# A new order in the front of a long-convolution and MLP kernel: load queues, a masked table, turns and norms on another engine, and both column means ahead of one stage

## The chip, the cores and the metric

The kernel runs on one core of a Trainium2 chip. A core has five engines that work side by side, each through its own list of instructions in order: TensorE (PE, matrix products into PSUM; its weight loads are shown as PEld), VectorE (DVE), ScalarE (ACT), GpSimd (POOL) and SyncE (SP). SyncE and ScalarE also issue DMA transfers; the two queues are shown as SPq and ACTq. Instructions wait for each other through semaphores.

The metric is the device time of one execution in microseconds (us), as the median of several runs. A profiled execution has its own time, and a span from its first to its last instruction.

## The reference, cut to what matters

```python
def _A_ref(q, k, v, shift_k, ssm_k, ssm_D):     # q: layernorm of the input x
    # k_shift: causal convolution of k along the sequence with 4 taps a channel
    for t in range(ks):
        k_shift = k_shift + k_pad[:, t:t + S, :] * shift_k[:, ks - 1 - t][None, None, :]
    kv = k_shift * v
    # y: causal convolution of kv along the sequence with ssm_k (by FFTs of length 2S), a channel each
    y = y + kv * ssm_D[None, None, :]
    return q * y

def _B_ref(x, w1, w2):
    return relu(x @ w1) @ w2

x = A_q
h = x + _A_ref(_layernorm(x), A_k, A_v, A_shift_k, A_ssm_k, A_ssm_D)
h2 = h + _B_ref(_layernorm(h), B_w1, B_w2)      # S = 2048, D = 512, Dff = 1376, bf16
```

## The kernel before

The convolution of length 4096 is done as a transform in two stages of matrix products with tables of sines, a product of spectra, and an inverse transform. The order on each engine is the order of the calls in the source (`tc.manual_schedule()`); there is no planner.

**Loads.** `load_rows(eng, rg)` loads `ssm_k`, 128 channels as a group `rg`, in two pieces of 256 KB (d = 0, 1) into the tile `kfl` in runs of 64 bf16. Group 1 and later group 3 go through ScalarE's queue, behind the small `wsh` (the 4 taps) and `drow` (ssm_D); groups 0 and 2 go through SyncE's queue. Then SyncE's queue carries, in this order: four transposing loads `kT` of `k` (`load_k`, L140 to L146), `vfl` (L112 to L116), the first rows of x (`qn0`, L161 to L163) between them, and `w1` (L154 to L159).

**Tables.** `f1f` is a small table of sines (ScalarE, L179) for stage 1. It is split in a bf16 high part `f1hi` and a low part `f1lo` (VectorE, L242 to L244), which GpSimd copies into `f1w` (`paired`, L253 to L257): a table that has the four groups of 32 partitions in one or the other of two column blocks, zero elsewhere. `drow2` (`spikes`) has ssm_D in the same layout. The larger table `tab` of stage 2 has 32 x 4 x 64 entries a partition: blocks 0 and 1 are sines of "turns" (`turns2`: integers on VectorE, a multiplication with addition at L184 and a mask at L185, then `sines2` on ScalarE); blocks 2 and 3 are their negatives (`negated`, GpSimd, L276). `inverse_turns` prepares tables of the inverse transform on GpSimd, `diagonals` the diagonal matrices `wdiag` of the 4 taps.

**Front.** `warm(13, ...)` runs products whose result nobody uses (L421). `s1(gb)` is stage 1 of ssm_k for one eighth of the channels: 4 products that add the spike of ssm_D (L350), 32 products on `kfl` and `f1w` (L358), and two copies out of PSUM, one on ScalarE and one on VectorE ("AD": first half on ACT, second on DVE; L317, L319). `tap(u)` is the 4-tap convolution of a chunk of k (L375) with a copy to `ksh`. `second_k(kp)` is stage 2 of ssm_k for a pair of frequencies (L388), with a copy back into `a1k` by the engine its letter names. It reads blocks 0 to 2 of `tab`; the products of x (`product`) also read block 3. All of these take PSUM tiles through `bank2`, in a fixed rotation of four tiles: the fourth tile before must have been copied out.

`row(q)` transposes a quarter of `ksh` (L333) and multiplies it by v into `xfl` (VectorE, L335). `bn_stats`, `moments` and `norm_rows(0, ...)` give the first layernorm of x. `column_means(m)` sums columns of w1 by products (L408), ScalarE copies them to `wm` (L410) and `center(n)` subtracts them from w1 on GpSimd (L414). Then stage 1 of x (`stage1(... xfl ...)`, L546) runs in eight steps, with the second half of the means and centers behind its first step.

**After that.** `product(kp)`, 16 times: two stage-2 products `u2` and `u1`, then the spectra are multiplied, `u2` on VectorE (L575), `u1` on GpSimd from a copy by ScalarE (L574, L580) for ten of the sixteen and on VectorE for the others. The inverse transform, the gate, the second layernorm and the MLP (`mlp1`, `mlp2`) follow.

Of the kernel before, what the change touches and what calls it, by code (L numbers as in the profile page):

```python
# [9 lines left out]
ALU = mybir.AluOpType  # L10
# [5 lines left out]
P = 128  # L16
# [39 lines left out]
def kernel(  # L56
# [37 lines left out]
    def first_channel(rg, d):  # L94
        return 128 * rg + 64 * (d ^ (rg % 2))
# [5 lines left out]

    kfl = front.tile([P, 64, 2, 64], BF16, name="kfl")

    def load_rows(eng, rg):
        for d in range(2):
            src = bass.AP(tensor=A_ssm_k.tensor, offset=A_ssm_k.offset + S * first_channel(rg, d), ap=[[64, 32], [S, 64], [1, 64]])
            eng.dma_start(out=kfl[32 * rg:32 * rg + 32, :, d, :], in_=src)


    vfl = front.tile([P, 64, P], BF16, name="vfl")  # L110

    def load_v(r):  # L112
        for d in range(2) if r % 2 else (0,):
            n = 64 if r % 2 else P
            src = bass.AP(tensor=A_v.tensor, offset=A_v.offset + first_channel(r, d), ap=[[64 * D, 32], [D, 64], [1, n]])
            nc.sync.dma_start(out=vfl[32 * r:32 * r + 32, :, 64 * d:64 * d + n], in_=src)  # L116

    zero = consts.tile([P, 512], BF16, name="zero")
    nc.vector.memset(zero[:], 0.0)
# [14 lines left out]
    def chunk(name):  # L134
        return front.tile([P, DC, CH + 16], BF16, tag="kT", name=name, bufs=4)


    tb = [chunk(f"tb{b}")[:].rearrange("p c t -> p (c t)").bitcast(I32)[:, 0:1024].rearrange("p (a b) -> p a b", b=64) for b in range(2)]

    def load_k(c):  # L140
        kT[c] = chunk("kT")
# [77 lines left out]
    f1f = early.tile([P, 64], F32, name="f1f")  # L219
    _sin(f1f[:, 0:32], t1[:, 0:32], 128)  # L220
    _sin(f1f[:, 32:64], t1[:, 32:64], 128, neg=True)
    load_rows(nc.scalar, 3)
    o2 = consts.tile([P, 2, 2], F32, name="o2")
    for i in range(2):
        for b in range(2):
            nc.vector.tensor_scalar(out=o2[:, i, b:b + 1], in0=n2c[:], scalar1=32.0 * i, scalar2=4096.0 + 2048.0 * b,
                                    op0=ALU.mult, op1=ALU.add)

    def turns2(i, b):
# [4 lines left out]
    ta00 = turns2(0, 0)  # L234
    ta01 = turns2(0, 1)
    f1hi = consts.tile([P, 64], BF16, name="f1hi")
    f1lo = consts.tile([P, 64], BF16, name="f1lo")
    f1d = early.tile([P, 64], F32, name="f1d")


    tab = tabp.tile([P, 32, 4, 64], F32R, name="tab")
# [27 lines left out]

    wm = rows.tile([P, 4, 344], F32, name="wm")  # L270

    def sines2(i, b, ta):
        _sin(tab[:, 16 * i:16 * i + 16, b, :], ta, 8192)
# [144 lines left out]
    def warm(n, data=zero[:], lhsT=None):  # L418
        ps = bank2("warm")
        for i in range(n):  # L420
            nc.tensor.matmul(out=ps[:, i % 2, :], lhsT=data[:, 0:P] if lhsT is None else lhsT, rhs=data, start=True, stop=True)  # L421
# [29 lines left out]
    def norm_rows(q, out, src):  # L451
        for i in range(4):
            t = 4 * q + i
            nc.vector.tensor_scalar(out=out[:, i, :], in0=src[:, i, :], scalar1=mv1[:, t, 0:1],
                                    scalar2=rstd1[:, t, :], op0=ALU.subtract, op1=ALU.mult)

    xfl = None
# [20 lines left out]
    spikes()  # L478
    sines2(0, 0, ta00)
    ta10 = turns2(1, 0)  # L480
    sines2(0, 1, ta01)
    ta11 = turns2(1, 1)
    diagonals()
    paired()
    negated(0)
    negated(1)
    sines2(1, 0, ta10)
    sines2(1, 1, ta11)
    load_k(2)
    load_k(3)  # L490
    load_v(0)
    load_v(2)
    load_x0()
    load_v(1)
    load_v(3)
    load_w1()
    negated(2)
    negated(3)
# [12 lines left out]
    tap(2, "A")  # L511
    second_k(0, "A")
    second_k(1, "D")
    second_k(2, "A")
    tap(3, "A")
    second_k(3, "D")
    second_k(4, "A")
    tap(4, "A")
    second_k(5, "D")
    pairs_pool()  # L520
    second_k(6, "A")
    tap(5, "D")
    nc.vector.bn_stats(out=st[:, 0, :], in_=qn0[:, 0, :])
    second_k(7, "A")
    tap(6, "A")
    nc.vector.bn_stats(out=st[:, 1, :], in_=qn0[:, 1, :])
    second_k(8, "A")
    tap(7, "D")
# [24 lines left out]

    late = pl.push("late")
# [300 lines left out]
```

## Time and profile before

| what | us |
|---|---|
| median of 3 runs (201.39 to 201.84) | 201.69 |
| the profiled execution's own time | 200.89 |
| its span | 199.1 |
| PE busy | 171.6 |
| DVE busy | 146.3 |
| ACT busy | 98.9 |
| POOL busy | 90.7 |

The chain that ended last, followed back from the last instruction, is TensorE for 66% of the span, VectorE for 21%, 5% "issue" (time in which an engine waited for nothing that the profile shows) and ScalarE for 3%. A mean over the whole span hides the stages: the MLP at the end is TensorE alone, while the front passes from loads to products to copies. So the views by time say more here than the totals: the chain in order of time, the timeline of an engine or a queue in a window, and the packets of a DMA queue in a window. In a chain line the columns are start, duration, engine, output tile, source line and count. In a timeline line they are start, duration, engine, line, operation, output and input tiles, count, and in brackets the idle time before it with what ended it.

### The profile page before, as it was taken

The page shows a single profiled execution, that of the slowest core. Times are in us where ns is not written, and L with a number is a line of the kernel's source. Part 1 is how long each engine was busy: PE and PEld are TensorE (multiplying, and loading weights), DVE is VectorE, ACT ScalarE, POOL GpSimd, SP SyncE. Part 2 cuts the span into 40 slices and gives each one's busy share as a digit, 9 for nine tenths or more (in the row PEclk, how much of TensorE's full clock was granted, in tenths as well). Part 3 has the DMA queues.
Part 4 walks back from the last instruction along what each step waited for, and adds up shares of the span by engine and source line. Part 5 has one row for each costly group of instructions (what it writes and reads, how often), then busy time and mean ns, then how long its engine had stood idle before and what let it go on. Part 6 is the DMA issues. An engine that isn't in the chain of part 4 may idle for free.

```text
span 199.1 us, 4079 instructions
## 1 busy us (share of the span) xinstructions
PE 171.6 (86%) x1638; PEld 109.1 (55%) x1643; DVE 146.3 (73%) x258; ACT 98.9 (50%) x113; POOL 90.7 (46%) x108
## 2 busy tenths in 40 slices
PE   0389989898986888888966999999999999999992
PEld 0137866496775777757744745445454444444451
DVE  7967866998667999999999869979966570471142
ACT  0387688931786588814995478003630164036300
POOL 7999983121991999992985520220220020002000
PEclk9999999999999999999999999999999999999999
DMA  7999998980000000008802622302511271120022
GB/s 117 216 242 198 193 203 133 203 174 0 3 3 3 0 5 0 3 0 221 200 0 53 201 86 44 59 12 64 112 29 26 61 102 27 40 58 8 3 54 53
DMA packets 51379, 15.99 MB, mean 80 GB/s; under 512 B 46784, under 2 KB 50208, under 8 KB 51360
## 3 DMA queue, kind: packets, MB, share of 16 engines
q1 hardware_dynamic: 42464, 14.61, 36.0%
q10 hardware_dynamic: 8896, 1.12, 3.7%
q8 instruction: 13, 0.21, 0.5%
q14 instruction: 6, 0.05, 0.1%
HBM read 9.64 MB, written 2.10 MB: 59 GB/s over the span
## 4 chain that ended last, share of the span: by engine, by line
PE 66%; DVE 21%; issue 5%; ACT 3%; ACTq 2%; POOL 1%; DVEq 0%; POOLq 0%
PE m L725 19%; PE m L780 18%; DVE a1x L575 7%; PE ps L358 6%; DVE zs L618 5%; PE u L388 4%; PE pkv L375 3%; PE ps2k L388 3%; PE pz L645 3%; PE warm L421 3%; DVE a1k L580 3%; PE pi L613 2%; ACT a1x L317 2%; DVE xfl L335 2%; PE pz L655 2%
## 5 line engine op out<-in xcount | busy, mean ns | idle before, releaser
L761 ACT ACTIVATE h1T<-m 128x512 bf16<-128x512 f32 (+1 forms) x44 | 25.9, 597 | 43.5 <-PE m L725 43.5
L725 PE MATMUL m<-hT,w 128*128 128x512 bf16 (+1 forms) x176 | 39.0, 379 | 0.2 <-ACT hT L692 0.2
L780 PE MATMUL m<-w,h1T 128*128 128x512 bf16 (+1 forms) x161 | 36.1, 379 | 0.2
L786 DVE SCALAR_TENSOR_TENSOR o<-m,rstd,hp 128x128 bf16<-128x128 f32 (+1 forms) x48 | 15.8, 389 | 25.6 <-PE m L780 24.8
L448 POOL TENSOR_SCALAR rstd<-mv 128x4 f32<-128x4 f32 x8 | 1.9, 232 | 64.4 <-DVE mv L446 64.4
L725 PEld LDWEIGHTS <-w 128*128 128x128 bf16 (+1 forms) x176 | 17.4, 100 | 20.5 <-issue 0.5
L780 PEld LDWEIGHTS <-h1T 128*128 128x128 bf16 (+1 forms) x165 | 15.9, 98 | 19.3 <-issue 0.3
L580 POOL TENSOR_TENSOR a1k<-usb,a1k 128x1024 fp32r<-128x1024 f32 x10 | 23.7, 2391 | 5.0 <-DVE a1x L575 5.0
L388 PE MATMUL u<-a1x,tab 64*128 64x256 f32 x256 | 18.8, 288 | 4.9 <-DVE a1k L580 2.4
L626 ACT CAST a1x<-zs 128x1024 fp32r<-128x1024 f32 (+2 forms) x10 | 17.3, 1730 | 10.8 <-DVE zs L618 10.8
L575 DVE TENSOR_TENSOR a1x<-u,a1k 128x1024 fp32r<-128x1024 f32 x16 | 19.1, 1218 | 2.7 <-PE u L388 2.7
L388 PEld LDWEIGHTS u<-a1x,tab 64*128 64x128 f32 x256 | 16.4, 185 | 6.9 <-PE u L388 3.1
L624 POOL CAST a1x<-zs 128x1024 fp32r<-128x1024 f32 (+1 forms) x8 | 15.7, 1975 | 7.6 <-DVE zs L618 7.6
L618 DVE STREAM_TRANSPOSE zs<-pi 128x1024 f32<-128x1024 f32 x16 | 18.4, 1216 | 0.5 <-PE pi L613 0.5
L613 PE MATMUL pi<-a1k,wd 128*128 128x512 f32 x32 | 13.3, 417 | 2.6 <-DVE zs L618 1.5
L414 POOL TENSOR_TENSOR w<-w,wm 128x1376 bf16<-128x1376 bf16 x4 | 11.2, 2839 | 6.5 <-ACT wm L410 6.5
L317 ACT CAST a1k<-ps2k 128x1024 fp32r<-128x1024 f32 x12 | 11.9, 1016 | 4.2 <-PE ps2k L388 4.1
L574 ACT COPY usb<-u 128x1024 f32<-128x1024 f32 x10 | 10.1, 1016 | 5.9 <-PE u L388 5.6
L613 PE MATMUL pi<-a1x,wd 128*128 128x512 f32 x32 | 12.8, 400 | 0.0
L319 DVE CAST a1k<-ps 128x1024 fp32r<-128x1024 f32 x8 | 9.6, 1223 | 4.2 <-PE ps L358 4.2
L421 PE MATMUL warm<-zero,wdiag 128*128 128x512 bf16 x13 | 5.1, 581 | 8.4 <-DVE drow L251 8.4
L388 PE MATMUL ps2k<-a1k,tab 64*128 64x256 f32 x128 | 10.5, 296 | 1.4 <-DVE a1x L575 0.8
(116 smaller groups left out, 278.3 us busy)
## 6 DMA issues: line engine op xcount, KB each, us to landing
xall<-in_A_q_dram SPq DMA_DIRECT2D x16, 128.0 KB, 3.5
out_dram<-o SPq DMA_DIRECT2D x62, 32.0 KB, 1.6
w<-in_B_w_dram SPq DMA_DIRECT2D x4, 344.0 KB, 6.1
w<-in_B_w_dram SPq DMA_DIRECT2D x1, 1280.0 KB, 6.4
kfl<-in_A_ssm_k_dram SPq DMA_DIRECT2D x4, 256.0 KB, 5.4
kfl<-in_A_ssm_k_dram ACTq DMA_DIRECT2D x4, 256.0 KB, 6.4
vfl<-in_A_v_dram SPq DMA_DIRECT2D x2, 512.0 KB, 7.3
vfl<-in_A_v_dram SPq DMA_DIRECT2D x4, 256.0 KB, 4.9
```

What stands on the lines that cost most here:

```text
L317: nc.scalar.copy(out=o, in_=i)
L388: nc.tensor.matmul(out=ps[:, d, 256 * i:256 * i + 256], lhsT=tab[rw, k1, b:b + 2, :].rearrange("p b k -> p (b k)"), rhs=a_in[rw, c, k1, :] ...
L575: nc.vector.tensor_tensor(out=spot(a1x, kp), in0=u2[:], in1=kk.bitcast(F32), op=ALU.mult)
L580: (nc.gpsimd if pool else nc.vector).tensor_tensor(out=kk, in0=(usb if pool else u1)[:], in1=kk.bitcast(F32), op=ALU.mult)
L613: nc.tensor.matmul(out=ps[:, b, :], lhsT=wd[:, m:m + 2, :].rearrange("p b k -> p (b k)"), rhs=src[:, d, 16 * b:16 * b + 16, c0:c0 + 32], s ...
L618: nc.vector.transpose(out=zs[:], in_=ps[:].rearrange("p b (k c) -> p c (b k)", c=32))
L624: nc.gpsimd.tensor_copy(out=o, in_=i)
L626: nc.scalar.copy(out=o, in_=i)
L725: nc.tensor.matmul(out=ps1[:fsz].rearrange("p (i t) -> p i t", i=4), lhsT=w1[:, c, fc * P:fc * P + fsz], rhs=hT[sc][:, c // 2, :, c % 2, : ...
L761: nc.scalar.activation(out=h1T[:fsz, fc, :], in_=ps1[:fsz], func=ACT.Relu)
L780: nc.tensor.matmul(out=ps2[:], lhsT=lhsT, rhs=w2[:ksz, fc, :], start=(fc == 0), stop=(fc == NFC - 1))
L786: nc.vector.scalar_tensor_tensor(out=of(o[:], d)[:, a], in0=ps[:, a], scalar=rstd2[:, t, :], in1=pair(hp[sc][:, d, i, :])[:, a], op0=ALU.m ...
```

## The change

Nine things, in the front alone:

1. `load_rows` takes one piece (d) at a time. ScalarE's queue begins with piece (1, 1), then `drow`, then (1, 0); behind the two activations of `f1f` it goes on with (3, 1), `wsh`, (3, 0). SyncE's queue begins with (0, 0), as before, and keeps its order.
2. A tile `pad` of 112 bf16 in `consts` makes up for tiles that went and came, so that the tiles behind it keep their addresses (`kfl` is at 40192, a multiple of 256, before and after).
3. `f1w` and `drow2` are made on VectorE by multiplication with a mask of two columns, in place of `f1hi`, `f1lo`, `f1d` and nine GpSimd operations and four VectorE copies.
4. The turns of the second half of `tab` (i = 1) are made on GpSimd, with the mask still on VectorE, in between stage 1's copies; their sines come in between the copies of `second_k`. They have a tile `tt` of their own instead of two of the `kT` buffers.
5. `negated` makes one block at a time; block 3 comes after the moments, block 2 where `second_k` needs it.
6. `inverse_turns` comes ahead of `diagonals` on GpSimd; the warm-up has 14 products on `f1w`.
7. The taps and `second_k` stand in another order, with other engines for their copies.
8. `norm_rows(0, ...)` runs on GpSimd.
9. `column_means(1)` and the centers 2 and 3 come ahead of the first step of x's stage 1.

```diff
-    def load_rows(eng, rg):
-        for d in range(2):
-            src = bass.AP(tensor=A_ssm_k.tensor, offset=A_ssm_k.offset + S * first_channel(rg, d), ap=[[64, 32], [S, 64], [1, 64]])
-            eng.dma_start(out=kfl[32 * rg:32 * rg + 32, :, d, :], in_=src)
+    def load_rows(eng, rg, d):
+        src = bass.AP(tensor=A_ssm_k.tensor, offset=A_ssm_k.offset + S * first_channel(rg, d), ap=[[64, 32], [S, 64], [1, 64]])
+        eng.dma_start(out=kfl[32 * rg:32 * rg + 32, :, d, :], in_=src)
...
-    nc.vector.memset(drow2[:], 0.0)
-    nc.scalar.dma_start(out=wsh[:], in_=A_shift_k.rearrange("(r p) j -> p r j", p=P))
+
+    consts.tile([P, 112], BF16, name="pad")
+    load_rows(nc.scalar, 1, 1)
+    load_rows(nc.sync, 0, 0)
     nc.scalar.dma_start(out=drow[0:P:16, :], in_=A_ssm_D.rearrange("(r g) -> r g", g=64))
-    load_rows(nc.scalar, 1)
-    for rg in (0, 2):
-        load_rows(nc.sync, rg)
+    load_rows(nc.sync, 0, 1)
+    load_rows(nc.scalar, 1, 0)
+    load_rows(nc.sync, 2, 0)
+    load_rows(nc.sync, 2, 1)
...
-    load_rows(nc.scalar, 3)
+    load_rows(nc.scalar, 3, 1)
+    nc.scalar.dma_start(out=wsh[:], in_=A_shift_k.rearrange("(r p) j -> p r j", p=P))
+    load_rows(nc.scalar, 3, 0)
...
+    tt = early.tile([P, 2, 16, 64], I32, name="tt")
+
     def turns2(i, b):
-        ta = tb[b] if i else early.tile([P, 16, 64], I32, tag="ta", name="ta", bufs=2)[:]
-        _turns(ta, r2, n2c[:], 8192, o2[:, i, b:b + 1])
-        return ta
...
-    nc.vector.tensor_copy(out=f1hi[:], in_=f1f[:])
-    nc.vector.tensor_tensor(out=f1d[:], in0=f1f[:], in1=f1hi[:], op=ALU.subtract)
-    nc.vector.tensor_copy(out=f1lo[:], in_=f1d[:])
+        t = tt[:, b]
+        (nc.gpsimd if i else nc.vector).tensor_scalar(out=t, in0=r2, scalar1=n2c[:], scalar2=o2[:, i, b:b + 1],
+                                                      op0=ALU.mult, op1=ALU.add)
+        if not i:
+            masked(b)
+
+    def masked(b):
+        nc.vector.tensor_single_scalar(out=tt[:, b], in_=tt[:, b], scalar=8191, op=ALU.bitwise_and)
+
+
+    mask = consts.tile([P, 2], F32, name="mask")
+    nc.vector.memset(mask[:], 0.0)
+    for rg in range(DC):
+        nc.vector.memset(mask[32 * rg:32 * rg + 32, rg % 2:rg % 2 + 1], 1.0)
 
     f1w = consts.tile([P, 2, 2, 64], BF16, name="f1w")
 
+    def paired():
+        for r in range(2):
+            nc.vector.tensor_scalar(out=f1w[:, 0, r, :], in0=f1f[:], scalar1=mask[:, r:r + 1], scalar2=None, op0=ALU.mult)
+        for r in range(2):
+            nc.vector.scalar_tensor_tensor(out=f1w[:, 1, r, :], in0=f1f[:], scalar=mask[:, r:r + 1], in1=f1w[:, 0, r, :],
+                                           op0=ALU.mult, op1=ALU.subtract)
+
     def spikes():
-        for rg in range(DC):
-            q = slice(32 * rg, 32 * rg + 32)
-            nc.vector.tensor_copy(out=drow2[q, rg % 2, :], in_=drow[q, :])
-
-    def paired():
-        nc.gpsimd.memset(f1w[:], 0.0)
-        for rg in range(DC):
-            for i, f in enumerate((f1hi, f1lo)):
-                nc.gpsimd.tensor_copy(out=f1w[32 * rg:32 * rg + 32, i, rg % 2, :], in_=f[32 * rg:32 * rg + 32, :])
+        for r in range(2):
+            nc.vector.tensor_scalar(out=drow2[:, r, :], in0=drow[:], scalar1=mask[:, r:r + 1], scalar2=None, op0=ALU.mult)
...
-    def negated(i):
-        nc.gpsimd.tensor_single_scalar(out=tab[:, 8 * i:8 * i + 8, 2:4, :], in_=tab[:, 8 * i:8 * i + 8, 0:2, :].bitcast(F32),
+    def negated(i, b):
+        nc.gpsimd.tensor_single_scalar(out=tab[:, 8 * i:8 * i + 8, 2 + b, :], in_=tab[:, 8 * i:8 * i + 8, b, :].bitcast(F32),
                                        scalar=-1.0, op=ALU.mult)
...
+    turns2(0, 0)
+    paired()
+    spikes()
+    turns2(0, 1)
+    sines2(0, 0)
     load_k(0)
...
     inverse_turns()
-    warm(13, lhsT=wdiag[:, 0, 0:2].rearrange("p j g -> p (j g)"))
+    diagonals()
+    negated(0, 0)
+    negated(1, 0)
+    turns2(1, 0)
+    warm(14, lhsT=f1w[:, 0].rearrange("p r c -> p (r c)"))
+    sines2(0, 1)
     s1(0, "AD")
     s1(1, "AD")
+    turns2(1, 1)
     s1(2, "AD")
-    tap(0, "A")
     s1(3, "AD")
-    s1(4, "AD")
-    tap(1, "D")
+    s1(4, "DA")
     s1(5, "AD")
+    tap(0, "D")
     s1(6, "AD")
-    s1(7, "AD")
-    tap(2, "A")
+    masked(0)
+    s1(7, "DA")
+    tap(1, "A")
+    tap(2, "D")
     second_k(0, "A")
+    sines2(1, 0)
+    masked(1)
+    tap(3, "A")
     second_k(1, "D")
+    sines2(1, 1)
+    negated(2, 0)
+    negated(3, 0)
     second_k(2, "A")
-    tap(3, "A")
-    second_k(3, "D")
...
+    second_k(10, "A")
     moments(mv1, rstd1, 0)
-    second_k(9, "A")
+    negated(0, 1)
+    negated(1, 1)
+    negated(2, 1)
+    negated(3, 1)
+    norm_rows(0, qn0, qn0, nc.gpsimd)
     row(0)
-    second_k(10, "D")
-    norm_rows(0, qn0, qn0)
     second_k(11, "A")
     row(1)
     row(2)
     row(3)
     column_means(0)
+    column_means(1)
     for n in (0, 1):
+        center(n)
+    for n in (2, 3):
         center(n)
...
-        if gb == 0:
-            column_means(1)
-            for n in (2, 3):
-                center(n)
```

In the part of the order that is left out, the new calls run: second_k(2, "A"), tap(4, "D"), second_k(3, "A"), tap(5, "A"), second_k(4, "D"), second_k(5, "A"), the mask and sine of the inverse tables, tap(6, "A"), second_k(6, "D"), tap(7, "A"), second_k(7, "A"), then second_k(8), (9) and (10), all "A", with the four `bn_stats` between them.

More of the change, by code (lines that the diff above doesn't have):

```diff
@@ L102, with load_v @@
     kfl = front.tile([P, 64, 2, 64], BF16, name="kfl")
-    def load_rows(eng, rg):
-        for d in range(2):
-            src = bass.AP(tensor=A_ssm_k.tensor, offset=A_ssm_k.offset + S * first_channel(rg, d), ap=[[64, 32], [S, 64], [1, 64]])
-            eng.dma_start(out=kfl[32 * rg:32 * rg + 32, :, d, :], in_=src)
+    def load_rows(eng, rg, d):
+        src = bass.AP(tensor=A_ssm_k.tensor, offset=A_ssm_k.offset + S * first_channel(rg, d), ap=[[64, 32], [S, 64], [1, 64]])
+        eng.dma_start(out=kfl[32 * rg:32 * rg + 32, :, d, :], in_=src)
     vfl = front.tile([P, 64, P], BF16, name="vfl")
[L112 to L116, printed above, removed]
+    def load_v(eng, r, d):
+        n = 64 if r % 2 else P
+        src = bass.AP(tensor=A_v.tensor, offset=A_v.offset + first_channel(r, d), ap=[[64 * D, 32], [D, 64], [1, n]])
+        eng.dma_start(out=vfl[32 * r:32 * r + 32, :, 64 * d:64 * d + n], in_=src)
     zero = consts.tile([P, 512], BF16, name="zero")
@@ L135, in chunk @@
         return front.tile([P, DC, CH + 16], BF16, tag="kT", name=name, bufs=4)
-    tb = [chunk(f"tb{b}")[:].rearrange("p c t -> p (c t)").bitcast(I32)[:, 0:1024].rearrange("p (a b) -> p a b", b=64) for b in range(2)]
     def load_k(c):
@@ L227 @@
                                     op0=ALU.mult, op1=ALU.add)
+    tab = tabp.tile([P, 32, 4, 64], F32R, name="tab")
+    tt = early.tile([P, 2, 16, 64], I32, name="tt")
     def turns2(i, b):
-        ta = tb[b] if i else early.tile([P, 16, 64], I32, tag="ta", name="ta", bufs=2)[:]
-        _turns(ta, r2, n2c[:], 8192, o2[:, i, b:b + 1])
-        return ta
[L234 to L237, printed above, removed]
@@ L474, in seconds @@
             second_k(kp, eng)
+    turns2(0, 0)
[3 more added lines that the diff above has]
+    sines2(0, 0)
     load_k(0)
     load_k(1)
[L478 to L488, printed above, removed]
     load_k(2)
     load_k(3)
-    load_v(0)
-    load_v(2)
+    load_v(nc.sync, 0, 0)
+    load_v(nc.sync, 2, 0)
     load_x0()
-    load_v(1)
-    load_v(3)
+    load_v(nc.sync, 1, 0)
+    load_v(nc.sync, 1, 1)
+    load_v(nc.sync, 3, 0)
+    load_v(nc.sync, 3, 1)
     load_w1()
-    negated(2)
-    negated(3)
     inverse_turns()
-    warm(13, lhsT=wdiag[:, 0, 0:2].rearrange("p j g -> p (j g)"))
+    diagonals()
[4 more added lines that the diff above has]
+    sines2(0, 1)
     s1(0, "AD")
     s1(1, "AD")
+    turns2(1, 1)
     s1(2, "AD")
-    tap(0, "A")
     s1(3, "AD")
-    s1(4, "AD")
-    tap(1, "D")
+    s1(4, "DA")
     s1(5, "AD")
+    tap(0, "D")
     s1(6, "AD")
-    s1(7, "AD")
-    tap(2, "A")
+    masked(0)
+    s1(7, "DA")
+    tap(1, "A")
+    tap(2, "D")
     second_k(0, "A")
+    sines2(1, 0)
+    masked(1)
+    tap(3, "A")
     second_k(1, "D")
+    sines2(1, 1)
+    negated(2, 0)
+    negated(3, 0)
     second_k(2, "A")
-    tap(3, "A")
-    second_k(3, "D")
-    second_k(4, "A")
-    tap(4, "A")
-    second_k(5, "D")
+    tap(4, "D")
+    second_k(3, "A")
+    tap(5, "A")
+    second_k(4, "D")
+    second_k(5, "A")
     pairs_pool()
-    second_k(6, "A")
-    tap(5, "D")
+    tap(6, "A")
+    second_k(6, "D")
+    tap(7, "A")
+    second_k(7, "A")
     nc.vector.bn_stats(out=st[:, 0, :], in_=qn0[:, 0, :])
-    second_k(7, "A")
-    tap(6, "A")
+    second_k(8, "A")
     nc.vector.bn_stats(out=st[:, 1, :], in_=qn0[:, 1, :])
-    second_k(8, "A")
-    tap(7, "D")
+    second_k(9, "A")
     nc.vector.bn_stats(out=st[:, 2, :], in_=qn0[:, 2, :])
     nc.vector.bn_stats(out=st[:, 3, :], in_=qn0[:, 3, :])
+    second_k(10, "A")
     moments(mv1, rstd1, 0)
-    second_k(9, "A")
+    negated(0, 1)
[3 more added lines that the diff above has]
+    norm_rows(0, qn0, qn0, nc.gpsimd)
     row(0)
-    second_k(10, "D")
-    norm_rows(0, qn0, qn0)
     second_k(11, "A")
```

10 lines of the change are left out of this document (4 added, 6 removed).

## The prediction

> **What bounds the kernel now.** I read the chain of waits in order of time first, then the timeline of the two DMA queues, then the packets of each queue in slices of 0.2 to 0.4 us, then each engine's timeline around the seams. Chain (start, duration, what):
>
> ```profile
> 8.44 5.15 PE warm L421 x13
> 13.59 0.33 PE ps L350 x4
> 13.92 0.05 PE ps L358
> 13.96 0.76 issue
> 14.72 1.05 PE ps L358 x31
> ...
> 27.98 0.30 issue
> 28.27 1.68 PE ps2k L388 x24
> ...
> 49.15 0.14 issue
> 49.29 1.09 PE ps L358 x32
> 50.37 1.27 PE pm L408 x8
> 51.65 1.15 PE ps L358 x32
> ...
> 61.84 1.22 PE u L388 x16
> ```
>
> The edit lies wholly ahead of the first product at 61.84; from there to the end at 199.1 the program is the old one, and its transfers start when earlier work frees a buffer, so it should slide as a whole. Four marks split the front: ssm_k's stage 1 (14.72), second_k(0) (28.27), x's stage 1 (49.29), product (61.84).
>
> The 0.76 us of "issue" at 13.96 is a transfer: TensorE has done the first product of h=0 and stands before h=1, rows 2 and 3 of ssm_k. The queues (start, duration of the issue) and the packets of one slice, 11.6 to 12.0 and 13.2 to 13.6 (packets, MB, share):
>
> ```profile
> 0.72 5.80 SPq L107 DMA_DIRECT2D kfl<-in_A_ssm_k_dram  x4
> ...
> 2.41 2.71 ACTq L107 DMA_DIRECT2D kfl<-in_A_ssm_k_dram  x2
> ...
> 6.57 4.82 SPq L144 DMA_TRANSPOSE kT<-in_A_k_dram  x1
> 7.78 2.37 ACTq L107 DMA_DIRECT2D kfl<-in_A_ssm_k_dram  x1
> ```
> ```profile
> q1 hardware_dynamic: 451, 0.12, 126.8%
> ```
> ```profile
> q10 hardware_dynamic: 681, 0.09, 138.3%
> ```
>
> q1 is SP's, q10 ACT's. A 256 KB piece of ssm_k is 2,048 packets, 1.2 us at 681 in 0.4. The pieces go over the engines whole and by turns: SP, SP, ACT, SP, ACT, SP, ACT; then SP's transpose of kT0 (10.4 to 12.9), and only then ACT's last piece (12.8 to 14.1), and stage 1 goes on 0.6 later.
>
> w1 is the last load, and column_means needs it:
>
> ```profile
> 37.44 1.25 SPq L159 DMA_DIRECT2D w<-in_B_w_dram  x2
> ```
> ```profile
> DMA to landing us min/median/max: 7.2/7.2/7.2
> ```
>
> Its last issue starts at about 38.05, so it lands at 45.25; today the first mean starts at 47.05 and doesn't feel it.
>
> **The change part by part.**
>
> *ssm_k's rows.* Both queues now start at 0.72 with ssm_k; wsh goes from the head of ACT's queue to between ACT's last two pieces. First packets come at 1.75, as now. Eight pieces and wsh (512 packets, 0.3): 1.75 + 8 x 1.2 + 0.3 = 11.65, + 0.6 = **12.25**. The other bound has kT0 (2.15) ahead of the last piece again: 14.4. I take the first: an issue returns when the piece before it is half through, and kT0's packets came 1.5 to 1.8 us after the middle of SP's fourth piece (8.9). That middle is now 1.75 + 6.5 x 1.2 = 9.55, so kT0 comes at 11.1 to 11.4, while ACT's last piece stands only behind wsh; the piece behind the small drow returned in 0.36 us and is ready by 10. kfl stays at address 40192 in both builds, so its alignment is priced at nothing. One queue alone moves 150 to 181 GB/s (2.4 to 4.0 us), two 216, so some of the gain is from ACT's idle start. The Trainium skill, "DMA: Bandwidth & Descriptors", section "Issuing engines are not separate DMA queues", says that a second issuing engine saves only issue time; by it the rate alone would give nothing and only the order of the pieces would count. The rates just given speak against it here, for 128-byte packets.
>
> *First table by masks.* Nine GpSimd operations for f1w (10.04 to 13.88) and three VectorE ones (L242 to L244) go; four 128x64 ones of VectorE come, by L243's 0.23 each, and five memsets of 0.1. VectorE: o2 ends at 3.95, masks 4.45, one table of turns (0.81 + 0.69) 5.95. f1f needs ScalarE's table load (1.28), which stands behind ACT's third issue: 3.4 instead of 5.13, so f1f at 5.3. f1w's first half is there at 6.4 and the warm-up, now on f1w and not on wdiag, runs 14 products, 5.15 + 0.3, to 11.9. Stage 1 therefore starts at 12.3: **-2.4** (bounds -0.3 and -2.8).
>
> *Stage 1 with its taps.* TensorE does the same 8 stages and 3 taps; the taps move to the end. VectorE's list sets it: 1.15 until the first copy, 8 copies x 1.23, one tap 1.22, the mask of turns(1,0) 0.69: 12.9 to second_k(0) against 13.55 now, **-0.65**: 25.2. The two taps behind s1(7) cover the 0.30 of issue and the wait on VectorE's copy ahead of second_k(0).
>
> *Turns on GpSimd.* Its list now: inverse_turns (24.93 to 31.97 now, 7.05) from 7.2 to 14.25; wdiag with its ident2 2.9 to 17.2; two halves of L276 at 2.78/2 to 20.0; two turns by L307's 1.21 to 22.4. Tap 0 needs wdiag at about 19.6, the mask needs the first turns at 23.3. The cover is 2 us; without it VectorE's s1(7) copy and second_k(0) stand behind the mask, us for us.
>
> *Middle.* ScalarE takes nearly all copies: second_k(0) (0.6), then 9 copies x 1.01, two sines x 1.09, w's 0.46, 11.7 to the copy of second_k(7), whose PSUM tile row(0) takes: 37.5 (TensorE's own list, 11 x 0.6 + 5, ends at 36.8). Rows: 1.64, second_k(11) 0.6, three at 4.56: 44.3, last xfl 1.37: 45.7. norm_rows (4 x 0.41) and second_k(10)'s copy no longer stand between VectorE's xfl.
>
> *Both means ahead of x.* They'd run from 44.3, but w1 isn't there. SP's queue is one chain of issues, and its fourth piece is 0.65 later (9.55 for 8.9): w1 at 45.9. Six of the first mean's eight products (0.95) and the second mean (1.27): x's stage 1 at **48.15**, against 49.29. Bounds: w1 unmoved, 47.5; that chain another 1 us later, 49.15. From there the old stretch took 12.55 with the 1.27 mean and its ScalarE copy inside; without them the copies set it, about one VectorE copy (1.23) a stage with the double ScalarE step at stage 4: 11.6. Product at 59.75: **-2.1**.
>
> *norm and negations on GpSimd.* VectorE's copy of second_k(6) ends at 35.1, the statistics (4 x 0.68 + 0.37) at 38.2, rstd (0.23 + 1.04) at 39.5, four L276 halves to 45.1, four norm_rows. No row shows a 128x512 bf16 operation with two column scalars on GpSimd: L307 gives 0.6, L276 1.4. I take 1.0, between: 49.1; centers 11.24: 60.3, at worst 62. The first product needs GpSimd 2.66 after its start, at 62.4: hidden. The Trainium skill, "GPSIMD Engine Reference", section 3.1, gives 769 ns for a loop of 512 elements; by it the centers end at 59.4 and the sum is the same, but no run here shows it yet.
>
> **Sum.** Span 199.1 - 2.1 = 197.0; 1.8 lies around it, as 200.89 - 199.1 now: 198.8. The median of the runs is 0.8 above the profiled one, so **199.6**.
>
> **Rivals.**
> - *w1 is no bound:* SP's chain keeps its times. x at 47.5 or before, product 59.0, -2.8: 198.9. For it: transfers have gaps at 27 and 32 us. Against: four transposes at 3.06 each follow one another.
> - *kT0 gets ahead again:* stage 1 at 14.4, second_k(0) 27.3, rows done 46.4, means 48.9, product 60.55: -1.3, 200.4. For it: that is what happens now.
> - *Slower, by TensorE's clock:* with kT0 ahead the warm-up ends at 11.9 and TensorE stands 2.5 us. Gaps of 0.76, 0.90 and 1.55 (at 61.84) cost no pace, but none is longer. If the pace falls to that of the first warm products (0.427 for 0.22 to 0.3 us apart) for the 4.3 us that these took, some 2.1 are lost: -1.3 + 2.1 = +0.8, 202.5. It decides from a gap above 1.55. The Trainium skill, "TensorE: Matmul & The Clock Gate", Part 1, puts the fall after an idle window of about 3.4 us, which would spare this gap; no run here shows it.
> - *Slower, by w1:* each us that w1 lands after 45.9 is now one of x's stage 1, since both means are ahead. From 48.0 the kernel loses; a chain of SP 3 us longer gives 202.6. Against: transfers, sizes and slots are the same.
> - *No gain:* GpSimd is late. Its ten products of 2.39 have some 2 us of slack, so it must be free only after 66.5: norm_rows of 2.5 each, above every row. L257's copies did go from 0.23 to 0.78 beside VectorE's L184. 201.7.
>
> **How the numbers follow.** Forecast 0.45, w1 no bound 0.15, kT0 ahead 0.18, clock 0.07, w1 late 0.08, no gain 0.07. A change under 0.2% (0.4 us) can't be told from none. Faster 0.78, same 0.07, slower 0.15. The range takes the first three with their bounds and some of "no gain": 198.3 to 201.7; the forecast's own is 198.8 to 200.6.
>
> **What would show it.** ACT's last piece ahead of kT0's packets, s1 at 12.3 with warm-up done at 11.9; second_k(0) near 25.2; TensorE idle for about 1.5 us before column_means(0) with w1 as the reason, no second mean inside x's stage; product near 59.8; GpSimd's centers done before 62.4. A product at 61.8 or later makes the prediction wrong.

## The result, and the profile after

The changed kernel is slower: 203.50 us median (203.42 to 204.02 over 4 runs) against 201.54 for the kernel before beside it, a ratio of 1.010 [1.006, 1.014]. The profiled execution has a span of 201.6 against 199.1. The comparisons of times here leave out runs more than 1.5% above the fastest run of the same kernel; each verdict below is a ratio to the kernel before, with its 95% interval.

The chain of waits of the changed kernel, in order of time (start, duration, what):

```profile
6.38 5.70 PE warm L425 x14
12.07 0.33 PE ps L354 x4
12.40 1.00 PE ps L362 x32
...
25.35 0.69 PE ps2k L392 x8
...
39.49 4.94 POOL tab L280 x4
...
47.45 6.19 POOL qn L458 x3
53.64 11.19 POOL w L418 x4
64.85 1.02 ACT usb L587
```

The first half is what was wanted: the warm-up is over at 12.1, stage 1 of ssm_k runs on without the 0.76 of "issue", and second_k(0) is at 25.35 instead of 28.27. Then the chain passes to an engine that was not in it before. From 38.05 to 64.83 it is GpSimd: two small steps of the statistics, the negations of `tab`, the four norm_rows of line 458, the four centers of line 418. ScalarE's copy `usb` comes behind the last center, and TensorE behind that copy.

GpSimd's own timeline (start, busy us, line, operation, forms, count, and in brackets the idle time before with what ended it):

```profile
39.49 5.90 POOL L280 TENSOR_SCALAR tab<-tab 128x512 fp32r<-128x512 f32 x4
45.39 8.26 POOL L458 TENSOR_SCALAR qn<-qn,mv,rstd 128x512 bf16<-128x512 bf16 x4
53.61 11.21 POOL L418 TENSOR_TENSOR w<-w,wm 128x1376 bf16<-128x1376 bf16 x4
65.94 4.72 POOL L593 TENSOR_TENSOR a1k<-usb,a1k 128x1024 fp32r<-128x1024 f32 x2 [1.12 <-ACT usb L587]
```

Four norm_rows take 8.26, 2.07 each. GpSimd has no idle time from 39.49 to 64.82. In the kernel before, VectorE did the four norm_rows in 1.38, and GpSimd stood idle ahead of its centers:

```profile
44.07 1.38 DVE L454 TENSOR_SCALAR qn<-qn,mv,rstd 128x512 bf16<-128x512 bf16 x4
```
```profile
49.23 11.24 POOL L414 TENSOR_TENSOR w<-w,wm 128x1376 bf16<-128x1376 bf16 x4 [6.49 <-ACT wm L410]
```

ScalarE's timeline shows who pays, first in the kernel before, then in the changed one:

```profile
63.16 1.94 ACT L574 COPY usb<-u 128x1024 f32<-128x1024 f32 x2 [1.86 <-PE u L388]
```
```profile
64.85 1.93 ACT L587 COPY usb<-u 128x1024 f32<-128x1024 f32 x2 [4.38 <-POOL w L418]
```

The copy needs only TensorE's product, which began at 61.11. Yet it waits for a center, an operation on w1 that has nothing to do with it. The pool that holds the three `usb` buffers (bytes 118016 to 130304 of a partition) is opened where the pool with the means `wm` (125536 to 131040) was closed: the memory is reused, and the centers are the last readers of `wm`. The first `usb` buffer (118016 to 122112) does not itself touch `wm`; the program makes its copy wait all the same, for the fourth center.

TensorE's timeline at w1 and at the first product, and a table by stretches (length, TensorE's busy time with its count, those of its weight loads, VectorE, ScalarE and GpSimd, then the granted clock, the DMA share and GB/s):

```profile
45.86 3.75 PE L412 MATMUL pm<-w,ones 128*128 128x344 bf16 x14 [1.71 <-DMA w<-in_B_w_dram]
...
61.11 2.13 PE L392 MATMUL u<-a1x,tab 64*128 64x256 f32 x32 [1.66 <-ACT a1x L321]
...
65.92 1.10 PE L392 MATMUL u<-a1x,tab 64*128 64x256 f32 x8 [1.50 <-ACT usb L587]
```
```profile
46.00:49.00 3.00, 3.00 (x12) 1.53 (x11) 0.00 (x0) 0.73 (x1) 3.00 (x2) 0.50 0.03 5
...
66.00:69.00 3.00, 3.00 (x30) 3.00 (x32) 1.91 (x2) 1.79 (x2) 3.00 (x2) 0.51 0.00 0
...
103.00:106.00 3.00, 2.24 (x9) 2.21 (x10) 2.22 (x3) 2.73 (x2) 2.68 (x2) 0.61 0.00 0
```

w1 lands at 45.86, as forecast, but behind the gap the granted clock is 0.50, and 14 products take 3.75 that take 2.21 at full clock (below). The clock falls again behind the waits that end at 65.92 and at 103.76.

Four marks carry the account of every kernel here, in us of its profiled execution:

| kernel | ssm_k stage 1 in earnest | first product | GpSimd's first product | `pi` begins to run on | MLP's first product | span |
|---|---|---|---|---|---|---|
| before | 14.72 | 61.84 | 64.50 | 90.22 | 111.39 | 199.1 |
| changed | 12.24 | 61.11 | 65.94 | 91.71 | 113.81 | 201.6 |
| e1 | 12.35 | 59.05 | 61.71 | 87.45 | 109.48 | 197.2 |
| e2 | 14.73 | 61.26 | 63.92 | 89.64 | 110.81 | 198.6 |
| e5 | 12.77 | 62.08 | 64.75 | 90.48 | 111.71 | 199.6 |
| e9 | 12.56 | 60.48 | 63.16 | 88.90 | 110.14 | 197.8 |
| e10 | 14.89 | 63.07 | 65.74 | 91.48 | 112.83 | 200.8 |
| e11 | 12.63 | 58.59 | 61.61 | 87.00 | 109.08 | 196.8 |
| e12 | 14.70 | 60.63 | 63.29 | 89.03 | 110.26 | 198.0 |

From GpSimd's first product to `pi` it is 25.72 before, 25.77 in the changed kernel, 25.74 in e1 (e11: 25.39). So that product, not TensorE's, is the mark that the rest follows. The changed kernel is 1.44 later there than the kernel before. From `pi` to the MLP it takes 22.10 instead of 21.17, 0.93 more, where the clock fell at 103.76. 1.44 + 0.05 + 0.93 + 0.08 behind the MLP's first product are the 2.5 of the two spans.

### The profile page after: what moved, and what is told of

Same layout as the page of the kernel before. It is cut to its first block, busy times and chain, and to the rows that moved or that the text cites. A ratio compares the mean times of both kernels' runs of the same rounds, so it can differ in the third digit from the quotient of the medians.

```text
span 201.6 us, 4085 instructions
## 1 busy us (share of the span) xinstructions
PE 176.9 (88%) x1644; PEld 112.6 (56%) x1644; DVE 141.1 (70%) x254; ACT 99.1 (49%) x114; POOL 98.4 (49%) x109
## 3 DMA queue, kind: packets, MB, share of 16 engines
q10 hardware_dynamic: 8896, 1.12, 3.6%
## 4 chain that ended last, share of the span: by engine, by line
PE 59%; DVE 17%; POOL 13%; issue 6%; ACT 3%; DVEq 0%; POOLq 0%; ACTq 0%
PE m L738 19%; PE m L793 18%; POOL w L418 6%; DVE a1x L588 5%; DVE zs L631 5%; PE u L392 4%; POOL qn L458 3%; PE ps L362 3%; PE pz L658 3%; PE warm L425 3%; POOL tab L280 2%; PE pkv L379 2%; DVE a1k L593 2%; PE pz L668 2%; PE ps2k L392 2%
## 5 line engine op out<-in xcount | busy, mean ns | idle before, releaser
L392 PE MATMUL u<-a1x,tab 64*128 64x256 f32 x256 | 20.3, 300 | 5.9 <-DVE a1k L593 1.8
L392 PEld LDWEIGHTS u<-a1x,tab 64*128 64x128 f32 x256 | 17.5, 196 | 8.3 <-PE u L392 2.4
L626 PE MATMUL pi<-a1k,wd 128*128 128x512 f32 x32 | 13.8, 432 | 2.0 <-DVE zs L631 0.9
L280 POOL TENSOR_SCALAR tab<-tab 128x512 fp32r<-128x512 f32 x8 | 11.8, 1500 | 5.7 <-ACT tab L177 5.6
L321 ACT CAST a1k<-ps2k 128x1024 fp32r<-128x1024 f32 x13 | 12.8, 1033 | 1.7 <-PE ps2k L392 1.7
L323 DVE CAST a1x<-ps 128x1024 fp32r<-128x1024 f32 x7 | 8.3, 1220 | 7.4 <-PE ps L362 7.4
```

What stands on the lines that cost most here:

```text
L323: nc.vector.tensor_copy(out=o, in_=i)
L392: nc.tensor.matmul(out=ps[:, d, 256 * i:256 * i + 256], lhsT=tab[rw, k1, b:b + 2, :].rearrange("p b k -> p (b k)"), rhs=a_in[rw, c, k1, :] ...
L626: nc.tensor.matmul(out=ps[:, b, :], lhsT=wd[:, m:m + 2, :].rearrange("p b k -> p (b k)"), rhs=src[:, d, 16 * b:16 * b + 16, c0:c0 + 32], s ...
```

## The experiments

Theory A: what loses is the four norm_rows on GpSimd, at 2.07 each, through the centers behind them; everything ahead of them is the gain that was forecast.

**e1: norm_rows(0) back on VectorE, all else as changed.**

```diff
-    norm_rows(0, qn0, qn0, nc.gpsimd)
     row(0)
...
     row(3)
+    norm_rows(0, qn0, qn0)
```

> The changed kernel with norm_rows(0) back on VectorE, after the last row. Theory A: the four norms on GpSimd (8.3 us) put the centers at 53.6 to 64.9, and ScalarE's usb copy and the products wait for them. Then the centers end near 60, the first usb copy stands at about 62.4 instead of 64.85, GpSimd's first product near 63.8, and the span falls by 2.2 from 201.6 to 199.4 (198.4 if the clock's fall at 104 goes too); ratio to before 0.995 to 1.002. Rival B: the loss is in the front, w1's wait and both means at half clock; then the span stays above 200.9 and the ratio above 1.006.

198.66 median, ratio 0.985 [0.981, 0.989]. Timelines of TensorE, of GpSimd and of ScalarE:

```profile
45.33 2.21 PE L412 MATMUL pm<-w,ones 128*128 128x344 bf16 x14 [1.18 <-DMA w<-in_B_w_dram]
...
59.05 2.13 PE L392 MATMUL u<-a1x,tab 64*128 64x256 f32 x32 [1.66 <-POOL w L418]
```
```profile
47.23 11.24 POOL L418 TENSOR_TENSOR w<-w,wm 128x1376 bf16<-128x1376 bf16 x4 [1.82 <-ACT wm L414]
```
```profile
60.36 1.93 ACT L587 COPY usb<-u 128x1024 f32<-128x1024 f32 x2 [1.96 <-PE u L392]
```

The centers now wait for the means (1.82) instead of coming late to them, they end at 58.47, and `usb` waits for its product. (The center named at the product's 1.66 is not its cause: it ended 0.58 before, and the same 1.66 stands there in the changed kernel behind ScalarE's last copy.) One line moved back turns a loss of 1.0% into a gain of 1.5%. That is more than A expected (0.995 to 1.002), and not all of it is the edit's: GpSimd's first product comes 4.23 earlier (61.71 for 65.94), of which 2.17 is its wait behind the late centers and 2.06 is x's stage 1 (47.48 for 49.54), where w1 landed 0.5 earlier and the clock did not fall.

**e2: the kernel before, with norm_rows(0) alone on GpSimd.**

```diff
     moments(mv1, rstd1, 0)
+    norm_rows(0, qn0, qn0, nc.gpsimd)
...
-    norm_rows(0, qn0, qn0)
```

> The kernel before with norm_rows(0) alone moved to GpSimd. Theory A (a norm of 128x512 costs GpSimd 2.06 wherever it stands): 8.2 us from 42.7, centers 51.0 to 62.2, just in time for the usb copy; VectorE is rid of 1.38 in the rows, so the span is 197.8 to 199.3. Rival: the 2.06 came from the neighbours in the changed kernel; then each norm takes 0.6 to 1.4 here and the centers end near 60.5 as before.

200.82 median, ratio 0.998 [0.995, 1.000]. GpSimd's timeline:

```profile
42.86 8.27 POOL L454 TENSOR_SCALAR qn<-qn,mv,rstd 128x512 bf16<-128x512 bf16 x4
51.10 11.25 POOL L414 TENSOR_TENSOR w<-w,wm 128x1376 bf16<-128x1376 bf16 x4
```

The price is the same, but here the negations are done before, so the centers end at 62.35, against a first product at 61.26 that needs GpSimd at 63.92. It fits, and it costs nothing. A expected a span of 197.8 to 199.3; it is 198.6. So the move is not bad in itself: it is bad behind four negations of 5.9 that the same change put there (the norm_rows start at 45.39 instead of 42.86), and with a product that the change wanted earlier.

**e3: e1 with eight unused products ahead of the first mean**, to keep TensorE busy while w1 lands.

```diff
+    warm(8)
     column_means(0)
```

> e1 with 8 unused 128x512 products on TensorE between the last row and the first mean, where it waits 1.7 us for w1. Theory C (this wait drops TensorE's granted clock to half, and the means run cold): the 14 means after the wait take 2.2 instead of 3.75, the clock stays at 1.0 there, x's stage 1 starts at 48.1 to 48.3 instead of 49.5, and the span is 1.2 to 1.5 below e1's. Rival: the means are slow for w1's sake or the fall comes from somewhere else; then the same span as e1 within 0.4.

199.39 median, ratio 0.989 [0.985, 0.993], not told apart from e1. Neither profile shows a fall of the clock at the means, so there was nothing to save, and the filler puts all sixteen products of the means behind it, at 45.42, where e1 goes on at 45.33 with two of them done: x's stage 1 at 47.85 against 47.48.

**e4: what GpSimd takes for a tensor_scalar of 128x512**, 18 of them put into the MLP of the kernel before, two of each kind; they are work added that the outputs don't need.

```diff
+    price(qn0[:, 1, :], zero[:], ca, cb, ALU.subtract, ALU.mult)
+    price(qn0[:, 2, :], zero[:], ca, cb, ALU.mult, ALU.add)
+    price(qn0[:, 3, :], zero[:], 0.5, 2.0, ALU.subtract, ALU.mult)
+    price(fl[:, 512:1024], fl[:, 0:512], ca, cb, ALU.subtract, ALU.mult)
...
```

> The kernel before with 18 unused GpSimd operations of 128x512 during the MLP, in pairs: bf16 in place, bf16, other operators, constants for columns, bf16 to f32, f32, f32 to bf16, int32. It overwrites qn0 and rf after their last use, and the output is that of the reference. Theory: 4.0 ns an element for bf16 with two columns (2.06 each) wherever it is; int32 0.6 to 0.7. What differs tells what the row of int32 misled about: a floating-point operand, the subtraction, or writing in place. Rival: 2.06 was contention or in-place writing, and bf16 takes 0.6 to 1.4 here.

GpSimd's instructions that write `qn`, and those that touch `rf` (count, then ns min/median/max, first and last start, forms):

```profile
L825 POOL TENSOR_SCALAR qn<-zero,mv,rstd x4: 767/1421/2074, 151.5 to 156.6; 128x512 bf16<-128x512 bf16 x4
L825 POOL TENSOR_SCALAR qn<-qn,mv,rstd x2: 2072/2078/2083, 147.2 to 149.4; 128x512 bf16<-128x512 bf16 x2
L825 POOL TENSOR_SCALAR qn<-zero x2: 1922/1922/1922, 157.4 to 159.4; 128x512 bf16<-128x512 bf16 x2
L825 POOL TENSOR_SCALAR qn<-rf,mv,rstd x2: 2072/2072/2073, 171.6 to 173.8; 128x512 bf16<-128x512 f32 x2
```
```profile
L825 POOL TENSOR_SCALAR rf<-rf,mv,rstd x6: 767/768/2073, 165.7 to 177.9; 128x512 f32<-128x512 f32 x4, 128x512 int32<-128x512 int32 x2
```

The first line holds two pairs of one shape: subtract then multiply takes 2.07, multiply then add 0.767. In f32 it is 2.07 and 0.767 as well, in int32 multiply then add takes 0.767. Neither the type, nor writing in place, nor columns against constants (1.92) makes the price; the pair of operators does. Which of the two it is, or their order, was not tried. The Trainium skill, "GPSIMD Engine Reference", section 3.1, has 769 ns for a loop of 512 elements: the trace agrees for multiply then add, and for subtract then multiply it is off by 2.7 times.

**e5: the changed kernel, with the same norm_rows on GpSimd written as x * rstd + (-mean * rstd).**

```diff
-    norm_rows(0, qn0, qn0, nc.gpsimd)
+    nc.gpsimd.tensor_tensor(out=nmr[:], in0=mv1[:, 0:4, 0:1], in1=rstd1[:, 0:4, :], op=ALU.mult)
+    nc.gpsimd.tensor_single_scalar(out=nmr[:], in_=nmr[:], scalar=-1.0, op=ALU.mult)
+    for t in range(4):
+        nc.gpsimd.tensor_scalar(out=qn0[:, t, :], in0=qn0[:, t, :], scalar1=rstd1[:, t, :], scalar2=nmr[:, t, :],
+                                op0=ALU.mult, op1=ALU.add)
```

> The changed kernel with the four norms still on GpSimd, but as x times rstd plus a column of -mean times rstd (two more operations of 128x4). Theory A, sharpened: it is the pair subtract-then-multiply that costs 2.07 an operation (multiply-then-add cost 0.77 beside it), so the norms end near 49.5 instead of 53.6, the centers near 60.5 instead of 64.9, and the span is 197.2 to 199.0; ratio to before 0.984 to 0.992. Rival: GpSimd is the wrong engine whatever the operators, the norms take over 6 in all again and the span stays above 200.5.

200.14 median over ten runs (197.54 to 202.28), ratio 0.987 [0.982, 0.991]. GpSimd's timeline and TensorE's:

```profile
46.44 3.02 POOL L552 TENSOR_SCALAR qn<-qn,rstd,nmr 128x512 bf16<-128x512 bf16 x4
49.56 11.24 POOL L418 TENSOR_TENSOR w<-w,wm 128x1376 bf16<-128x1376 bf16 x4
```
```profile
46.81 3.77 PE L412 MATMUL pm<-w,ones 128*128 128x344 bf16 x14 [2.22 <-DMA w<-in_B_w_dram]
```

0.76 each. The work stayed on the engine that the change chose, no product or copy waits for it, and by the ratio the kernel gains what e1 gains; by the median over all ten runs it gains 0.5%. The profile is of a run of 201.43, with w1 at 46.81 and the clock down behind the wait: x's stage 1 at 50.52, so the span of 199.6 lies above A's 197.2 to 199.0, and below the rival's 200.5. With the norm_rows out of the way it is w1 that x's stage 1 waits for, and w1's landing differs from profile to profile by 2; that may be why ten runs of e5 spread over 4.7, where four of the changed kernel lie within 0.6.

**e6, e7, e8: the falls of the clock.** e6 is e1 with seven unused products ahead of the first product of the last transform (`pz`); e7 and e8 are the kernel before with a warm-up of 30 and of 24 products instead of 13, which move all later work. They test theory D, that the clock follows a beat counted from the program's start, so that the place of a gap decides.

```diff
+            warm(7)
             last(0, 0, pool=1)
...
-    warm(13, lhsT=wdiag[:, 0, 0:2].rearrange("p j g -> p (j g)"))
+    warm(30, lhsT=wdiag[:, 0, 0:2].rearrange("p j g -> p (j g)"))
```

> e1 with 7 unused products in the gap of 1.9 ahead of the first product of the last transform, where the granted clock fell to half at 99.8. Theory C (an idle gap takes the clock): no fall there, these products take 1.2 instead of 2.0, and the span is 196.1 to 196.6 against 197.2. Rival: the fall comes from something else and stays, or the filler delays the products behind it; then 197.0 or more.

> The kernel before with 30 warm-up products, everything later by about 2.6. By theory D the gap now ends near 104.8, which is 101.4 plus one beat: no fall, span 201.7. If gaps take the clock by chance or by the kernel alone, this run can't be told from e8 in its clock.

> The kernel before with 24 instead of 13 warm-up products, which moves everything behind by about 1.3. Theory D: whether a gap of 1.9 takes the clock hangs on where it lies in a beat of some 3.4 that starts with the program; gaps that ended at 99.5 and 103.8 took it, those that ended at 101.6 and 102.2 did not. The gap now ends near 103.5: the clock falls there, and the span is 199.1 + 1.3 + 0.9 = 201.3. Rival (the fall belongs to the changed order): no fall, 200.4.

e6: ratio 0.986 [0.975, 0.997], not told apart from e1: inconclusive on the time, though its profile shows no fall at the filled gap; as seven of thirteen unfilled gaps show none either, that alone says little. In e8 the gap ends at 103.91, near the 103.76 of the changed kernel, and nothing falls (clock 1.00 in the whole run); in e7 it ends at 105.48, where D has no fall, and the clock falls. D is refuted as put, a beat that starts with the program; the last section comes back to it.

**e9: e1 with the second mean and the centers 2 and 3 behind x's first step**, as in the kernel before.

```diff
     column_means(0)
-    column_means(1)
     for n in (0, 1):
         center(n)
-    for n in (2, 3):
-        center(n)
...
+        if gb == 0:
+            column_means(1)
+            for n in (2, 3):
+                center(n)
```

> The changed kernel with norm_rows(0) on VectorE after row(3), and with column_means(1) and center(2), center(3) put back behind x's first step, where the kernel before has them. Theory A (the price and place of the four norm_rows were the whole loss; both means ahead are worth a little): TensorE still waits for w1 behind row(3) (1.2 to 2.2 as w1 lands), then 8 means of 1.1 to 1.3 instead of 14, x's stage 1 some 1.0 earlier, but its eight second means fall into it: the product of the first transform within 0.5 of 59.05, time 198.0 to 199.8. Rival E (the means ahead are a loss, since TensorE has nothing but the wait for w1 before them): product 0.7 or more earlier than 59.05, time below 198.0. Rival F (putting them back costs the 0.6 to 1.1 that the change won there, as the late centers reach into the product): product at 60 or later, time 199.8 or more.

200.74 median over ten runs (198.94 to 202.76), ratio 0.993 [0.989, 0.996], product at 60.48: by its numbers F's, but not by F's cause. The centers end at 59.95, ahead of the product, and w1 landed 1.5 later than in e1's profile. From w1's landing to the first product it is 13.65, against 13.72 in e1: the place of the second mean is worth 0.07 there, which is nothing.

**e10: e1 with the loads in their old order; e12: the same with norm_rows(0) on VectorE between row(1) and row(2).**

```diff
-    load_rows(nc.scalar, 1, 1)
-    load_rows(nc.sync, 0, 0)
+    nc.scalar.dma_start(out=wsh[:], in_=A_shift_k.rearrange("(r p) j -> p r j", p=P))
     nc.scalar.dma_start(out=drow[0:P:16, :], in_=A_ssm_D.rearrange("(r g) -> r g", g=64))
-    load_rows(nc.sync, 0, 1)
     load_rows(nc.scalar, 1, 0)
+    load_rows(nc.scalar, 1, 1)
+    load_rows(nc.sync, 0, 0)
+    load_rows(nc.sync, 0, 1)
...
-    load_rows(nc.scalar, 3, 1)
-    nc.scalar.dma_start(out=wsh[:], in_=A_shift_k.rearrange("(r p) j -> p r j", p=P))
     load_rows(nc.scalar, 3, 0)
+    load_rows(nc.scalar, 3, 1)
```

> The changed kernel with norm_rows(0) on VectorE after row(3), and with the loads in the order of the kernel before (SP and ACT as they were, ssm_k behind the others). Theory A (the order of loads moves the start of the rows by the 0.7 to 0.9 that the traces of before and after show, and w1's landing sets x's first stage in either): s1 of ssm_k starts at 12.8 to 13.2 instead of 12.0, rows done 0.6 to 1.0 later, so TensorE's wait for w1 shrinks to 0.2 to 0.6 and x's stage 1 starts within 0.4 of 47.48; time within 0.6 of the 198.66 of that kernel. Rival G (the loads are worth their whole shift to the end): time 199.3 to 200.0, x's stage 1 at 48.2 or later.

e10: 202.47 median over ten runs (201.56 to 209.11), ratio 1.001 [0.997, 1.005]. Both expectations missed the time: stage 1 starts in earnest at 14.89, the means end at 48.7 with no wait for w1 (x's stage 1 at 48.66, as G had it), but x's second stage waits 2.12 for VectorE, and the product comes at 63.07, 4.0 behind e1. The norm_rows on VectorE, in e10:

```profile
L458 DVE TENSOR_SCALAR qn<-qn,mv,rstd x4: 395/425/2930, 47.6 to 48.6; 128x512 bf16<-128x512 bf16 x4
```

The last of the four took 2.93 instead of 0.40. It started at 48.6, just behind GpSimd's first center (48.41 to 51.42), and ended at 51.57, just behind that center's end. The Trainium skill, "SBUF — State Buffer", section "SBUF: two separate sides", says that GpSimd and VectorE share a pair of ports, and that a GpSimd operation, or a VectorE operation in a two-port mode, which starts first holds the pair for its whole instruction; this row agrees, but the norm_rows beside GpSimd's negations in e12 (0.71 at most, a negation is 1.5) do not. e12 takes the collision away.

> The old order of loads once more, as in e10, but with norm_rows(0) on VectorE between row(1) and row(2), where GpSimd is still at its negations, and not behind row(3), where one of the four took 2.93 in e10 beside GpSimd's centers. Theory A (that collision and the clock fall behind it were what made e10 lose 4 us at the product; the loads themselves are worth what w1's landing leaves of them, 1.2 at x's stage 1): all four norm_rows at 0.39 to 0.48, no wait of 2 us in x's stages, x's stage 1 at 48.5 to 49.3, product at 60.0 to 61.0, 1.0 to 2.0 behind the 59.05 of e1; time 199.6 to 200.9. Rival G (the loads are worth their whole shift of 2.5 at the end): product at 61.5 or later, time 201.0 or more.

```profile
L458 DVE TENSOR_SCALAR qn<-qn,mv,rstd x4: 408/562/714, 44.6 to 45.9; 128x512 bf16<-128x512 bf16 x4
```

199.92 median, ratio 0.993 [0.990, 0.996]; the wait of 2.12 is gone, x's stage 1 at 49.08, product at 60.63 (e1: 59.05). Two of the norm_rows beside the negations still take 0.71, so A's bound of 0.48 was too tight; its marks and time hold. The new order of loads, worth 2.35 at stage 1 (14.70 against e1's 12.35), is worth 1.3 to 1.6 behind w1 (199.92 - 198.66 by the medians, 60.63 - 59.05 by the product): e12's means wait for nothing, e1's wait 1.18 for w1. Of the 1.6, 0.55 is a wait of x's stage 1 for `xfl`, which the norm_rows in their earlier place push back, so the loads alone may be worth less.

**e11: e5 with the means apart as in e9.**

> The changed kernel with its four norm_rows kept on GpSimd but written as x * rstd + (-mean * rstd), multiply then add, and with column_means(1), center(2) and center(3) behind x's first step. Theory A (0.77 each leaves GpSimd free by 49.6, the centers end by 62, the copy of usb waits for no center): time 197.5 to 199.8, product at 58.5 to 60, with no wait of ScalarE's usb copy for w's line. Rival: the second pair of centers, released later, ends behind 62.5 and the usb copy waits for it as in the changed kernel: product at 60 to 61.5, time 200 to 201.5.

199.01 median (198.10 to 199.70), ratio 0.986 [0.980, 0.992], as e1 and e5. TensorE's and ScalarE's timelines:

```profile
44.77 1.05 PE L412 MATMUL pm<-w,ones 128*128 128x344 bf16 x6 [0.32 <-DMA w<-in_B_w_dram]
```
```profile
60.52 1.93 ACT L593 COPY usb<-u 128x1024 f32<-128x1024 f32 x2 [2.73 <-POOL w L418]
```

The time and the product are A's, but its "no wait of `usb`" is wrong. The centers end at 60.49, the copy begins 1.93 behind the product instead of 1.31, and GpSimd's first product 3.02 behind it instead of 2.66; `pi` is on time all the same (28.41 from the product, 28.40 in e1). That measures the slack at GpSimd's first product: at least 0.36.

Not tried: `wm` and `usb` in separate memory, which would give the false wait a price by itself.

## Why the prediction was wrong

Forecast 199.6 (198.3 to 201.7), measured 203.5. Its span was 197.0, the measured one is 201.6. By its own steps:

- **ssm_k's rows, the first table, stage 1: right.** Stage 1 from 12.01 (12.3), warm-up done at 12.1 (11.9), second_k(0) at 25.35 (25.2). ACT's last piece went ahead of kT0, as argued. e12 and e1 bear out that this comes from the order of the loads. One reading in this step was wrong, though the sum did not use it: "One queue alone moves 150 to 181 GB/s". Those are slices at 2.4 to 4.0, the first two with small packets of ACT's queue among them; at 8.8 to 9.2 SP's queue alone moved 218 in the same kernel, and the step's own line of 681 packets in 0.4 us is one queue alone at 218, where two moved 216. So these rates do not speak against that statement of the Trainium skill.
- **Middle and rows: right**, row(0) at 37.07 (37.5), last xfl done at 45.2 (45.7).
- **w1 and both means: the landing right (45.86 for 45.9), its spread not seen.** Over six profiled runs with the new loads, w1 came between 44.77 and 46.83. The landing is therefore one draw out of two us, not a point. The second part of the step, means of 2.2, held in e1; in the changed kernel the clock fell behind the wait and they took 3.75. It cost 1.5 at TensorE's product and, by the rows, nothing at the end, since GpSimd was later still.
- **norm_rows at 1.0 each: the step that failed.** The prediction said: "I take 1.0, between: 49.1; centers 11.24: 60.3, at worst 62." Each took 2.07, outside both bounds (0.6 and 1.4). The norm_rows ended at 53.6 and the centers at 64.82. The bounds came from rows with other operators (multiply and add; multiply alone), and e4 shows that on GpSimd it is the operators that set the price. e5 and e11, which change them and leave the norm_rows on GpSimd, win 1.3% and 1.4% against the kernel before.
- **"some 2 us of slack" for GpSimd: wrong as well.** By it, centers at 64.82 would still have been hidden, as GpSimd "must be free only after 66.5". But its products follow one another in pairs with idle gaps of 0.16 to 0.28 in the kernel before, under 1.0 in all, so a late first one makes all late: 25.72 to 25.77 from it to `pi`, whatever came before. In e11 a start 0.36 later behind TensorE's product cost nothing at `pi`; in the changed kernel one 2.17 later (4.83 for 2.66) came through whole (30.60 from the product to `pi`, 28.40 in e1).
- **The wait of `usb` was not in it.** Behind the centers came not GpSimd's product but ScalarE's copy (1.02) for it, held by reused memory. GpSimd's first product started at 65.94 instead of 62.4; this 3.5, with the late product and the late centers in it, is most of the 4.6 us by which the span missed. How much of it the copy's wait alone costs was not tried: GpSimd stands 1.12 for the copy, and TensorE 1.50 (ahead of 65.92).
- **The gap ahead of the last transform, and the clock behind it: not in it**, 0.93. The gap is 1.9 in every kernel, and the clock falls behind it in six of the thirteen profiled kernels that have the gap as it was, e1 and e11 among them, so the change does not need to be its cause. That it has no part in it is not shown: all four runs of the changed kernel have a mean granted clock of 0.973 to 0.975, which is three falls of 3.41 at half clock in 201.6. The rival on the clock took gaps above 1.55 as what decides; here a fall followed one of 1.50 (ahead of 65.92), and none one of 1.66 (ahead of 61.11).

The rival "no gain" was the nearest: GpSimd late, at "norm_rows of 2.5 each, above every row", with a chance of 0.07. It had the right place and too much slack. What spoke against it, that every row lay below such a price, was no evidence, as no row showed the operation at all.

## What to carry to other kernels

Before work is moved to GpSimd, price it by a row with the same operators, not the same shape; where there is none, the bounds are wide, and the question is what stands behind the operation. Rewriting an affine step as multiply then add (0.77 for 2.07) was worth as much here as taking it off the engine, as far as the intervals tell (0.987 and 0.986 against 0.985). An engine's slack is read from the gaps in its own run of later work, and a tile in a pool over reused memory can inherit the last readers of what the closed pool held.

## What was unexpected of the hardware

- GpSimd, tensor_scalar of 128x512: 2.07 for subtract then multiply, 0.767 for multiply then add, the same in bf16 and f32.
- One VectorE norm_row of 0.40 took 2.93 beside a GpSimd center that started just before it (e10).
- The granted clock falls to 0.50 for 3.41 us at a time (6.83 in e4, behind a gap of 4.85) behind gaps in TensorE's work of 1.5 to 2.2 us, but not each time: behind w1 after 1.71, 2.22 and 2.15 (changed kernel, e5, e6), not after 2.14 (e9), 1.18 (e1) or 0.32 (e11). The Trainium skill, "TensorE: Matmul & The Clock Gate", Part 1, names an idle window of about 3.4 us; the length of the falls agrees, but these runs show falls after shorter gaps.
- Within one execution the falls start whole multiples of 3.413 apart: at 45.61, 66.09 and 103.64 in the changed kernel (6 and 17 of them), at 53.88 and 105.08 in e10 (15). With this beat laid over the nine profiles that have a fall behind a wait, TensorE was busy for 1.26 to 1.60 us of the beat ahead of ten of the twelve falls (1.95 and 0 ahead of the others), and for 1.75 or more of every other beat between the first products and the last. So where a gap lies in the beat seems to decide, and the beat's phase differs from run to run, which is what D had wrong; this is read from profiles, and no experiment set the phase.
